# Attention, MLP and routed experts on one core: both ends reordered, and the rows of the position bias dealt out differently

## The chip, the cores and the metric

The program runs on one NeuronCore of a Trainium2 chip. The metric is the device time of one execution in microseconds. The kernel before took 1055.13 us as the median of three runs (1053.98 to 1055.31).

## What is computed

Attention over 4 batches, 8 heads, 576 positions and head size 64, with a bias that depends on the two positions; then an MLP of 512 to 2048 to 512 with the gate h * sigmoid(1.702 h); then a routing of the 2304 tokens to 8 experts with 288 places each and a two-layer expert.

```python
scores = scale * np.matmul(q, k.transpose(0, 1, 3, 2))
psi_rel = np.log1p(np.abs(pos[:, None] - pos[None, :]))
psi_i = np.log1p(np.maximum(pos[:, None], 1.0))
x = (psi_rel / psi_i)[..., None]
bias = np.maximum(x @ w1 + b1, 0.0) @ w2          # 32 hidden units, 8 heads
scores = scores + bias.transpose(2, 0, 1)[None]
attn = softmax(scores);  x = np.matmul(attn, v)
g = h * sigmoid(1.702 * h), h = x @ w_in;  x = g @ w_out
# then each token goes to one of 8 experts: max(x @ w1[e], 0) @ w2[e]
```

## The kernel before

All is fp32. The bias is the same for all batches and is computed once, in 36 **groups** of 64 query positions. In a group the 128 partitions hold 4 positions times 32 hidden units, and there are four **rows** (`row(q, k)`, k = 0 to 3, line 123), each a 128x576 tile: a stretch of the table `lx` (the logarithms times w1), limited from below. A row is made on VectorE (L136, `max` against a column of `psi`) or on ScalarE (L134, Relu with a bias from `bpsi`); the two forms differ by a constant, which `cor` puts back. In the kernel before, ScalarE makes row 0 of the even groups and VectorE the rest: seven rows of a pair of groups on VectorE and one on ScalarE (`alone`, L122).

`prod(q)` (L143, matmuls L151) multiplies the four rows of group q by `w2b` into one two-bank PSUM tile, and `out(q)` (L155, L161 on ScalarE) reads that tile, adds `cor`, scales, and writes a 128x576 staging tile, from which SP's queue scatters it by DMA into the place where the bias waits for its scores (L166, L169). There are 12 row buffers, so a row of group q+3 waits until `prod(q)` has read the buffer, and 7 staging tiles.

The **table** is made at the start: `lx4` (4x1152) is loaded by DMA into a tile P whose borders POOL clears first, three matmuls with `sel` spread it over 128 partitions (L103), and three evictions multiply it by w1 (two on VectorE L107, one on ScalarE L105). Then come `bpsi` and `psi` (L111, L112), and the correction `cor` (four matmuls L116, three small VectorE operations). Ahead of these TensorE runs 12 warm-up matmuls on the identity, which POOL makes.

Attention runs in **slots**, one for each block of up to 128 query rows of a pair of heads (`slot`, L358). The first 20 slots belong to the first four head pairs and batches, in the order block 4 (64 rows, one score tile), then blocks 0 to 3 (two score tiles). One slot issues, each engine taking its own in this order: the transposes of the block three slots back (L294) with three evictions (ScalarE, VectorE, ScalarE); the exponentials of the block before (L257, ScalarE); the output of the last attention product (ScalarE L344, then VectorE L351); the scores of the new block (L237); the bias rows of group q+2 (`rows(0)`); the minimum of scores plus bias for each score tile (L249, VectorE, `least`), which frees the tile; the attention product (L321); then `prod(q)` and `prod(q+1)`, the rows of group q+3 (`rows(1)`) and `out(q)`, `out(q+1)`. Score tiles and bias products share one PSUM pool of two buffers (`sc_ps`). Six groups are multiplied before the first slot (a prologue loop), then two in each of the first 15 slots. Every engine works through its instructions in the order in which they are written; which of the two `sc_ps` buffers a tile gets is chosen when the program is built.

At the **end** the last expert makes its output in four blocks of 128 columns: product, eviction (L1270), three transposes into the banks `ops` (`back`, L1219), then copies into SBUF (`some`, L1230 VectorE and L1232 ScalarE) and three scatters by POOL (`outs`, L1237). For the last expert the copies take columns 0 to 383 after block 2 and 384 to 511 after block 3.

Of the kernel before, what the change touches and what calls it, by code (L numbers as in the profile page):

```python
# [24 lines left out]
NE = 8  # L25
# [39 lines left out]
class Bias:  # L65
# [3 lines left out]
    def __init__(self, net, cst, HL, B4, G9, more, bp, lx4, sc_ps, av_ps):  # L69
# [16 lines left out]
        nc.scalar.dma_start(w1c, bcast_dram(io["w1"], [[0, 4], [1, 32], [1, 1]]))
        nc.sync.dma_start(sel, io["c_sel"])
        nc.scalar.dma_start(b1c, bcast_dram(io["b1"], [[0, 4], [1, 32], [1, 1]]))
        nc.sync.dma_start(psi, bcast_dram(io["psi"], [[4 * NQ, 4], [0, 32], [1, 4 * NQ]]))
        nc.gpsimd.dma_start(w2r, bcast_dram(io["w2"], [[0, 4], [H, 32], [1, H]]))  # L90
# [7 lines left out]

        for c0, c1 in ((0, 320), (320, LXC), (LXC, LXW)):
            sl = slice(c0, c1)  # L100
            ps = sc_ps.tile([128, 2, 512], F32, name="sc")[:, 0, 0:c1 - c0] if c0 < LXC else \
                av_ps.tile([128, 512], F32, name="av")[:, 0:c1 - c0]
            nc.tensor.matmul(ps, sel, lx4[:, sl], start=True, stop=True)  # L103
            if c0 == 320:
                nc.scalar.activation(lx[:, sl], ps, AF.Copy, scale=w1c)  # L105
            else:
                nc.vector.tensor_scalar(lx[:, sl], ps, w1c, None, op0=OP.mult)  # L107
# [6 lines left out]
        cps = av_ps.tile([128, 320], F32, name="av")  # L114
        for k in range(4):
            nc.tensor.matmul(cps[32 * k:32 * k + 32, 0:1], w2b, b1c, start=True, stop=True)  # L116
        nc.vector.tensor_scalar(self.cor[1], cps[:, 0:1], 8.0, None, op0=OP.mult)
        nc.vector.tensor_copy(self.cor[0], self.cor[1])
        nc.vector.memset(self.cor[0][0:32], 0.0)
        self.X, self.PS = {}, {}  # L120

    def alone(self, q):  # L122
        return q % 2
# [54 lines left out]
def attention(net, cst, m, HL, G9, gall):  # L178
# [195 lines left out]

    for k in range(4):
# [4 lines left out]
        if k == 0:  # L380
            lx4 = P[0:4]
# [1029 lines left out]
```

## Time and profile before

| | before |
|---|---|
| median of 3 runs | 1055.13 us (1053.98 to 1055.31) |
| profiled execution | 1055.28 us, its span 1053.5 us, mean granted TensorE clock 0.989 |
| PE busy | 1018.3 us (97% of the span) |
| DVE busy | 704.7 us (67%) |
| ACT busy | 478.4 us (45%) |
| POOL busy | 238.2 us (23%) |

The span runs from the first to the last instruction; the execution is 1.8 us longer than the span. PE is TensorE's matmuls, DVE is VectorE, ACT is ScalarE. Matmuls are pipelined and their ends are modelled, so starts say more than ends. A bracket behind an instruction gives the idle time before it and what ended it.

### The profile page before, as it was taken

To read this page: it belongs to the slowest core of one execution; us is meant where nothing else is said; L and a number is where in the kernel's file an instruction comes from. 1 tells how busy PE (TensorE), PEld (TensorE's weight loads), DVE (VectorE), ACT (ScalarE), POOL (GpSimd) and SP (SyncE) were. 2 spreads that over 40 slices of the span, in tenths; PEclk is the share of its full clock that TensorE was granted. 3 is DMA by queue.
4 is the path that set the end of the run, shared out by engine and by line. 5 is a ranking of instruction groups with operands and counts; after the bars stand their busy time and mean duration, and the time that the engine had idled before them with its cause. 6 is when DMAs were issued, how large, how long until landed. Compare 5 with 4: busy or idle time off the path is not lost.

```text
span 1053.5 us, 19951 instructions
## 1 busy us (share of the span) xinstructions
PE 1018.3 (97%) x7689; PEld 799.3 (76%) x7689; DVE 704.7 (67%) x1838; ACT 478.4 (45%) x1036; POOL 238.2 (23%) x297
## 2 busy tenths in 40 slices
PE   8889999999998989999999999999999999999996
PEld 4455766666665767887777777777777999999996
DVE  6899666666667188874445788888886555555551
ACT  4677776767676223232224322222223455555552
POOL 1122343434344043331113200000001222222111
PEclk8999999999999999999999999999999999999998
DMA  6533422121200255632340272222223755566300
GB/s 185 141 92 100 133 69 71 35 72 35 89 1 1 54 205 210 225 138 103 130 130 17 70 238 83 81 81 81 81 81 133 253 184 184 200 206 205 103 24 23
DMA packets 75747, 119.74 MB, mean 114 GB/s; under 512 B 10340, under 2 KB 38272, under 8 KB 74116
## 3 DMA queue, kind: packets, MB, share of 16 engines
q1 hardware_dynamic: 70156, 104.81, 31.2%
q0 software_dynamic: 3136, 9.46, 2.9%
q10 hardware_dynamic: 2360, 4.20, 1.1%
q8 instruction: 60, 0.98, 0.4%
q14 instruction: 35, 0.29, 0.1%
HBM read 84.24 MB, written 23.60 MB: 102 GB/s over the span
## 4 chain that ended last, share of the span: by engine, by line
PE 68%; issue 19%; DVE 5%; POOL 4%; ACT 2%; DMA 2%; POOLq 0%; SPq 0%; DVEq 0%; ACTq 0%
PE yps L1071 19%; PE hps L609 17%; PE tr L294 8%; PE sc L237 8%; PE av L321 7%; PE sc L151 3%; POOL ye L1189 2%; POOL out_dram L1237 2%; PE rps L843 2%; DVE gall L136 2%; PE lacc L684 1%; DVE P L249 1%; DMA woraw<-in_moe_w_out_dram 1%; PE wps L663 1%; PE av L386 0%
## 5 line engine op out<-in xcount | busy, mean ns | idle before, releaser
L266 POOL TENSOR_SCALAR P<-P,r 128x576 f32<-128x576 f32 x144 | 107.9, 760 | 226.1 <-DVE r L264 164.4
L609 PE MATMUL hps<-xh 128*128 128x512 f32 (+1 forms) x640 | 148.6, 374 | 0.0
L257 ACT ACTIVATE P<-P,nm 128x576 f32<-128x576 f32 x144 | 111.2, 772 | 63.5 <-DVE nm L249 59.8
L609 PEld LDWEIGHTS hps<-xh 128*128 128x128 f32 x640 | 110.3, 188 | 26.9 <-issue 7.5
L1071 PE MATMUL yps<-xh,g 128*128 128x512 f32 x336 | 114.2, 403 | 0.0
L237 PE MATMUL sc<-k,q 64*128 64x288 f32 (+1 forms) x640 | 102.3, 429 | 1.1 <-ACT gall L161 1.1
L294 PEld LDWEIGHTS tr<-ident,P 128*128 128x128 f32 x736 | 79.2, 141 | 31.4 <-issue 25.5
L321 PE MATMUL av<-PT,v 128*64 128x128 f32 (+3 forms) x880 | 95.5, 350 | 4.3 <-DVE xl L351 1.6
L294 PE MATMUL tr<-ident,P 128*128 128x128 f32 x736 | 97.8, 278 | 0.0
L616 DVE TENSOR_TENSOR gall<-hps,sg 128x512 f32<-128x512 f32 (+1 forms) x77 | 48.0, 631 | 71.2 <-ACT sg L615 71.1
L1208 PE MATMUL mps<-xh 128*128 128x288 f32 x288 | 87.3, 303 | 0.0
L321 PEld LDWEIGHTS av<-PT,v 128*64 128x64 f32 x880 | 49.4, 136 | 47.4 <-issue 24.6
L1208 PE MATMUL mps<-xh,xl 128*128 128x288 f32 x288 | 85.1, 295 | 0.0
L1208 PE MATMUL mps<-xl,xh 128*128 128x288 f32 x288 | 84.8, 294 | 0.0
L1071 PE MATMUL yps<-xh 128*128 128x512 f32 x240 | 81.5, 400 | 0.8 <-DVE xh L516 0.8
L615 ACT ACTIVATE sg<-hps 128x512 f32<-128x512 f32 (+1 forms) x77 | 42.3, 551 | 87.8 <-PE hps L609 87.3
L609 PE MATMUL hps<-xl,xh 128*128 128x512 f32 (+1 forms) x320 | 78.9, 368 | 0.0
L270 ACT ACTIVATE PT<-tr 128x384 f32<-128x384 f32 (+2 forms) x176 | 73.0, 423 | 8.3 <-PE tr L294 8.0
L516 DVE TENSOR_TENSOR xl<-wo,xh 128x512 fp32r<-128x512 f32 (+1 forms) x56 | 51.2, 940 | 34.3 <-ACT xh L511 34.2
L237 PEld LDWEIGHTS sc<-k,q 64*128 64x128 f32 (+1 forms) x640 | 54.7, 176 | 25.5 <-issue 11.2
L1071 PEld LDWEIGHTS yps<-xh,g 128*128 128x128 f32 x336 | 63.0, 188 | 13.8
L1208 PE MATMUL mps<-yhi,xh 128*128 128x288 f32 x224 | 68.8, 307 | 0.0
(251 smaller groups left out, 2054.4 us busy)
## 6 DMA issues: line engine op xcount, KB each, us to landing
gd<-gall SPq DMA_DIRECT2D x12, 1152.0 KB, 5.4
woraw<-in_moe_w_out_dram SPq DMA_DIRECT2D x16, 512.0 KB, 5.0
wo<-in_moe_w_dram SPq DMA_DIRECT2D x4, 2048.0 KB, 8.2
gall<-in_moe_w_dram SPq DMA_DIRECT2D x8, 1024.0 KB, 5.0
wiraw<-in_moe_w_in_dram SPq DMA_DIRECT2D x14, 512.0 KB, 5.9
xl<-gd SPq DMA_DIRECT2D x18, 384.0 KB, 4.1
wiraw<-gd SPq DMA_DIRECT2D x18, 384.0 KB, 3.6
wo<-in_moe_w_dram SPq DMA_DIRECT2D x6, 1024.0 KB, 6.7
```

The costliest lines, as they stand in the source:

```text
L237: nc.tensor.matmul(out[:, hf, 0:288], q[rows, icol], k[rows, js[hf]], start=True, stop=True)
L257: nc.scalar.activation(Ps[hh], Ps[hh], AF.Exp, bias=nms[hh], scale=-1.0, accum_out=sums[:, hh:hh + 1])
L266: nc.gpsimd.tensor_scalar(p, p, r[:, hh:hh + 1], 1.0, op0=OP.mult, op1=OP.mult)
L270: nc.scalar.activation(out, in_, AF.Copy)
L294: nc.tensor.transpose(tr[:, k], P[:, c0:c0 + 128], ident)
L321: nc.tensor.matmul(ps[rows, :n], v[:, hh, jt], pt[:, 5 * hh + jt if jt < 4 else 4], start=jt == 0, stop=jt == NIT - 1)
L516: lo_eng.tensor_sub(lo, src, f(hi))
L609: nc.tensor.matmul(ps[:, :n], w[:, c], x[:, c, ts], start=k == 0, stop=k == len(seq) - 1)
L615: nc.scalar.activation(sg[:, :n], ps[:, :n], AF.Sigmoid, scale=1.702)
L616: nc.vector.tensor_tensor(out=self.gall[:, ft % NG, t0:t0 + n], in0=ps[:, :n], in1=sg[:, :n], op=OP.mult)
L1071: nc.tensor.matmul(ps, g[:, ft % 4], w(ft), start=k == 0, stop=k == 47)
L1208: nc.tensor.matmul(ps, w[:, c], x[:, c], start=k == 0, stop=k == len(seq) - 1)
```

## The change

Four edits. First, the start: the small loads are issued before anything else, in another order and on other queues (SP: lx, sel, b1, psi; ScalarE's: w1, w2; POOL's: only ipsi), `lx4` lies in the bias tile of block 4 and not in P, the warm-up matmuls read a tile of ones that VectorE clears, the third eviction of the table is put off to the rows of group 3 (`rest`), and the correction to the rows of group 1, with its PSUM from the pool of the transposes. Second, `alone` is always 0: row 0 of every group is made on ScalarE, so a pair of groups has six rows on VectorE and two on ScalarE. Third, in a slot only rows 0 and 1 of group q+2 are issued ahead of the minimums, and rows 2 and 3 and all of group q+3 behind the products (`part`). Fourth, the end: the last expert's copies are cut at columns 256 and 384, and its last block is transposed into three other PSUM tiles and copied by VectorE (two) and ScalarE (one).

```diff
+        pss = []
         for c0, c1 in ((0, 320), (320, LXC), (LXC, LXW)):
...
+            nc.tensor.matmul(ps, sel, lx4[:, c0:c1], start=True, stop=True)
+            pss.append(ps)
+        nc.vector.tensor_scalar(lx[:, 0:320], pss[0], w1c, None, op0=OP.mult)
+        nc.scalar.activation(lx[:, 320:LXC], pss[1], AF.Copy, scale=w1c)
...
+        def rest():
+            nc.vector.tensor_scalar(lx[:, LXC:LXW], pss[2], w1c, None, op0=OP.mult)
+
+        def correction():
+            cps = tr_ps.tile([128, 4, 128], F32, name="tr").rearrange("p a j -> p (a j)")
+            for k in range(4):
+                nc.tensor.matmul(cps[32 * k:32 * k + 32, 0:1], w2b, b1c, start=True, stop=True)
+            nc.vector.tensor_scalar(self.cor[1], cps[:, 0:1], 8.0, None, op0=OP.mult)
+            nc.vector.tensor_copy(self.cor[0], self.cor[1])
+            nc.vector.memset(self.cor[0][0:32], 0.0)
+        self.later = {1: correction, 3: rest}
...
     def alone(self, q):
-        return q % 2
+        return 0
...
     def rows(self, q):
+        if q in self.later:
+            self.later.pop(q)()
         if q < self.NQ:
             for k in range(4):
                 self.row(q, k)
+
+    def part(self, q, part):
+        for k in range(8):
+            if (k < 2) == (part == 0) and q + k // 4 < self.NQ:
+                self.row(q + k // 4, k % 4)
...
+    small = [B4[0:4, 0:2].rearrange("p h j -> p (h j)")]
+    nc.sync.dma_start(small[0], io["lx"])
+    nc.scalar.dma_start(small[3], bcast_dram(io["w1"], [[0, 4], [1, 32], [1, 1]]))
+    nc.sync.dma_start(small[1], io["c_sel"])
+    nc.sync.dma_start(small[4], bcast_dram(io["b1"], [[0, 4], [1, 32], [1, 1]]))
+    nc.scalar.dma_start(small[5], bcast_dram(io["w2"], [[0, 4], [H, 32], [1, H]]))
+    nc.sync.dma_start(small[2], bcast_dram(io["psi"], [[nq, 4], [0, 32], [1, nq]]))
...
+    nc.vector.memset(pts[0][:, 0:128], 1.0)
     for _ in range(NWARM):
-        nc.tensor.matmul(busy[:, 0:128], ident, ident, start=True, stop=True)
+        nc.tensor.matmul(busy[:, 0:128], pts[0][:, 0:128], pts[0][:, 0:128], start=True, stop=True)
...
-                    rows=lambda k: bias.rows(q + 2 + k), outs=lambda: [bias.out(q + k) for k in range(2)])
+                    rows=lambda k: bias.part(q + 2, k), outs=lambda: [bias.out(q + k) for k in range(2)])
...
+            ps = [t[:, 128 * m:128 * m + 128] for t in OM[e]]
+            if e == NE - 1 and m == 3:
+                ps = [mps.tile([128, 288], F32, name="mps")[0:96, 128 * k:128 * k + 128] for k in (0, 1)]
+                ps.append(tps.tile([128, 288], F32, name="tps")[0:96, 0:128])
...
-                if r == 1:
+                if (r == 1) == (src is None):
                     nc.vector.tensor_copy(o, ps)
...
-                if m == 3 and e == NE - 1:
-                    some(e, 0, 384)
+                if m > 1 and e == NE - 1:
+                    some(e, *((0, 256) if m == 2 else (256, 384)))
...
-        back(NE - 1, 3)
-        some(NE - 1, 384, DM)
+        some(NE - 1, 384, DM, back(NE - 1, 3))
```

## Rows read from the trace of the kernel before

**Rows 1.** Stretches, core 0: length, busy us (instructions) by engine, granted clock, DMA.
```profile
10.00:23.60 13.60, 12.17 (x124) 6.26 (x128) 13.34 (x33) 8.38 (x12) 0.00 (x0) 0.79 0.64 194
23.60:43.86 20.26, 17.01 (x178) 7.93 (x180) 17.51 (x44) 12.54 (x25) 2.47 (x3) 0.92 0.65 176
44.67:106.61 61.94, 55.55 (x692) 34.88 (x692) 57.10 (x150) 46.60 (x101) 13.93 (x19) 1.00 0.37 97
112.24:300.00 187.76, 187.76 (x1451) 121.08 (x1450) 120.50 (x387) 129.02 (x342) 72.72 (x99) 1.00 0.21 66
```

**Rows 2.** Chain that ended last, in one slot: start us, us, what.
```profile
74.09 0.94 DVE gall L136 x2
75.03 0.67 DVE P L249
```

**Rows 3.** Timeline of PE: start us, us, instruction, count, idle before.
```profile
69.46 2.15 PE L151 MATMUL sc<-gall,w2b 128*32 128x288 f32 x32 [0.49 <-DVE nm L249]
72.67 1.24 PE L237 MATMUL sc<-k,q 64*128 64x288 f32 x8
73.84 1.31 PE L321 MATMUL av<-PT,v 128*64 128x128 f32 x20
75.77 2.15 PE L151 MATMUL sc<-gall,w2b 128*32 128x288 f32 x32 [0.61 <-DVE nm L249]
106.61 2.15 PE L151 MATMUL sc<-gall,w2b 128*32 128x288 f32 x32
```

**Rows 4.** Timeline of ACT, the same slot.
```profile
70.78 0.83 ACT L161 ACTIVATE gall<-sc,cor,ipsi 128x576 f32<-128x576 f32 x1 [1.42 <-PE sc L151]
71.68 0.83 ACT L161 ACTIVATE PT<-sc,cor,ipsi 128x576 f32<-128x576 f32 x1
72.41 0.76 ACT L257 ACTIVATE P<-P,nm 128x576 f32<-128x576 f32 x1
73.17 0.26 ACT L344 ACTIVATE xh<-av 128x128 fp32r<-128x128 f32 x1
74.82 0.78 ACT L134 ACTIVATE gall<-gall,bpsi 128x576 f32<-128x576 f32 x1
```

**Rows 5.** Timeline of DVE, the same slot.
```profile
73.46 0.29 DVE L351 TENSOR_TENSOR xl<-av,xh 128x128 fp32r<-128x128 f32 x1
76.96 2.28 DVE L136 TENSOR_SCALAR gall<-gall,psi 128x576 f32<-128x576 f32 x4 [0.31 <-PE sc L151]
```

**Rows 6.** Timeline of the start, PE, SP's queue and DVE.
```profile
1.36 4.83 PE L386 MATMUL av<-ident 128*128 128x128 f32 x24 [1.36 <-POOL ident masks.py:199]
1.51 0.38 SPq L382 DMA_DIRECT2D P<-in_lx_dram  x1
6.96 0.55 DVE L107 TENSOR_SCALAR gall<-sc,w1c 128x320 f32<-128x320 f32 x1 [6.96 <-PE sc L103]
8.36 0.75 DVE L107 TENSOR_SCALAR gall<-av,w1c 128x512 f32<-128x512 f32 x1 [0.84 <-PE av L103]
9.30 0.29 DVE L112 TENSOR_SCALAR psi<-psi,b1c 128x144 f32<-128x144 f32 x1
10.38 12.97 DVE L136 TENSOR_SCALAR gall<-gall,psi 128x576 f32<-128x576 f32 x30
```

**Rows 7.** Timeline: outputs of groups 2 and 3, and the first minimum.
```profile
16.86 1.62 ACT L161 ACTIVATE PT<-sc,cor,ipsi 128x576 f32<-128x576 f32 x2
23.60 0.76 DVE L249 CUSTOM_DVE_ANT_0 P<-sc,b 128x576 f32<-128x576 f32 x1 [0.26 <-DMA xh<-PT]
```

**Rows 8.** Timeline of PE in the first slots.
```profile
23.51 1.18 PE L151 MATMUL sc<-gall,w2b 128*32 128x288 f32 x16 [1.03 <-ACT PT L161]
25.74 2.14 PE L237 MATMUL sc<-k,q 64*64 64x288 f32 x8 [1.05 <-ACT gall L161]
```

**Rows 9.** Timeline of the end, PE and POOL.
```profile
1044.29 0.70 PE L1219 MATMUL ops<-ident,oT 128*96 128x128 f32 x3 [0.60 <-ACT o L1232]
1045.19 0.92 POOL L1237 DMA_INDIRECT out_dram<-o,perm  x1 [21.34 <-ACT o L1232]
```

More of the change, by code (lines that the diff above doesn't have):

```diff
@@ L65, with __init__ @@
 class Bias:
-    def __init__(self, net, cst, HL, B4, G9, more, bp, lx4, sc_ps, av_ps):
+    def __init__(self, net, cst, HL, B4, G9, more, bp, small, sc_ps, av_ps, tr_ps):
         self.net, self.HL, self.B4 = net, HL, B4
@@ L77, in __init__ @@
         lx = self.lx = G9[:, 0:LXW]
-        sel = bp.tile([4, 128], F32, name="sel")
-        psi = self.psi = bp.tile([128, 4 * NQ], F32, name="psi")
+        lx4, sel, psi, w1c, b1c, w2r = small
+        self.psi = psi
         ipsi = self.ipsi = bp.tile([128, NQ], F32, name="ipsi")
-        w1c = bp.tile([128, 1], F32, name="w1c")
-        b1c = bp.tile([128, 1], F32, name="b1c")
         w2b = self.w2b = bp.tile([128, 32], F32, name="w2b")
-        w2r = bp.tile([128, NE], F32, name="w2r")
         nc.gpsimd.memset(w2b, 0.0)
[L86 to L90, printed above, removed]
         nc.gpsimd.dma_start(ipsi, io["ipsi"])
@@ L113, in __init__ @@
         self.cor = [bp.tile([128, 1], F32, name=f"cor{k}") for k in range(2)]
[L114 to L119, printed above, removed]
+        def rest():
[8 more added lines that the diff above has]
+        self.later = {1: correction, 3: rest}
         self.X, self.PS = {}, {}
     def alone(self, q):
-        return q % 2
+        return 0
     def row(self, q, k):
@@ L373, in slot @@
             avq.add(av(*tj))
+    bp = es.enter_context(net.pool("bp", side="right"))
+    nq = 4 * len(GROUPS)
+    small = [B4[0:4, 0:2].rearrange("p h j -> p (h j)")]
+    small += [bp.tile(shape, F32, name=n) for n, shape in (("sel", [4, 128]), ("psi", [128, nq]), ("w1c", [128, 1]),
+                                                           ("b1c", [128, 1]), ("w2r", [128, NE]))]
+    nc.sync.dma_start(small[0], io["lx"])
[4 more added lines that the diff above has]
+    nc.sync.dma_start(small[2], bcast_dram(io["psi"], [[nq, 4], [0, 32], [1, nq]]))
     for k in range(4):
@@ L379, in attention @@
             nc.gpsimd.memset(P[:, c:c + 64], 0.0)
-        if k == 0:
-            lx4 = P[0:4]
-            nc.sync.dma_start(lx4, io["lx"])
     busy = av_ps.tile([128, 320], F32, name="av")
+    pts = [ptp.tile([128, 9 * 320], F32, name="PT") for _ in range(2)]
+    nc.vector.memset(pts[0][:, 0:128], 1.0)
     for _ in range(NWARM):
-        nc.tensor.matmul(busy[:, 0:128], ident, ident, start=True, stop=True)
-    pts = [ptp.tile([128, 9 * 320], F32, name="PT") for _ in range(2)]
+        nc.tensor.matmul(busy[:, 0:128], pts[0][:, 0:128], pts[0][:, 0:128], start=True, stop=True)
     pta = [pts[0][:, 9 * 128 * k:9 * 128 * (k + 1)] for k in range(2)]
     more = [pts[1][:, S * k:S * k + S] for k in range(5)]
-    bp = es.enter_context(net.pool("bp", side="right"))
-    bias = Bias(net, cst, HL, B4, G9, more, bp, lx4, sc_ps, av_ps)
+    bias = Bias(net, cst, HL, B4, G9, more, bp, small, sc_ps, av_ps, tr_ps)
     for pi in range(B):
@@ L1217, in back, with some @@
             o = OT.pop((e, m))
+            ps = [t[:, 128 * m:128 * m + 128] for t in OM[e]]
+            if e == NE - 1 and m == 3:
+                ps = [mps.tile([128, 288], F32, name="mps")[0:96, 128 * k:128 * k + 128] for k in (0, 1)]
+                ps.append(tps.tile([128, 288], F32, name="tps")[0:96, 0:128])
             for r in range(3):
-                nc.tensor.transpose(OM[e][r][:, 128 * m:128 * m + 128], o[:, 96 * r:96 * r + 96], ident)
+                nc.tensor.transpose(ps[r], o[:, 96 * r:96 * r + 96], ident)
+            return ps
         O = {}
-        def some(e, c0, c1):
+        def some(e, c0, c1, src=None):
             if c0 == 0:
@@ L1227, in some @@
             for r in range(3):
-                o, ps = O[e][r][:, c0:c1], OM[e][r][:, c0:c1]
-                if r == 1:
+                o, ps = O[e][r][:, c0:c1], src[r] if src else OM[e][r][:, c0:c1]
+                if (r == 1) == (src is None):
                     nc.vector.tensor_copy(o, ps)
```

6 lines of the change are left out of this document (removed).

## The prediction
> **What bounds the kernel now.** I read the stretches first, then the chain, then the engines' timelines of one slot. From 112 us on TensorE has no idle time at all for 188 us [rows 1], so what is won or lost ahead of that point reaches the end in full, unless a later stage waits for something else. Ahead of it lie three stages where TensorE does not set the pace. In the prologue (10.0 to 23.6) VectorE is busy 13.34 of 13.60 us. In the four slots of block 4 (23.60 to 43.86) it is busy 17.51 of 20.26, and TensorE and ScalarE take turns in waiting. In the next ten slots (44.67 to 106.61, 6.19 us each) VectorE is busy 57.10 of 61.94, TensorE 55.55, ScalarE 46.60 [rows 1]. The chain there runs through bias rows on VectorE, the minimum, and then the products [rows 2]; TensorE stands idle 0.49 to 0.61 us ahead of each pair of products until VectorE's minimum frees the PSUM [rows 3]. So the second and third edits act on the engine that bounds. At the very end the last transposes wait 0.60 us for ScalarE's copies [rows 9].
>
> **The start.** Before, SP's first load waits until 1.51 us for POOL to clear P, and the warm-up matmuls wait 1.36 us for the identity [rows 6]. Both waits go. How much earlier VectorE can have its ones ready is not shown: between 0 and 1.36 us; I take 0.4, since VectorE too has to start up. SP issues one load more (b1) ahead of psi and q and k, ScalarE's queue has w2 in place of b1, POOL's loses w2. None of the landings is shown; the latest moment at which psi and b1 are there is the operation that reads them, at 9.30 us [rows 6]. In order on VectorE, the first eviction starts at 6.96 and the third at 8.36, because the third waits for TensorE; psi follows 0.94 after that start and takes 0.29 [rows 6]. With the third put off, and the first 0.20 shorter, the first row starts 0.94 - 0.20 + 0.30 = 1.04 us after the first eviction: 6.96 - 0.40 + 1.04 = 7.6 us, where it is 9.95 now (one row spacing of 12.97 / 30 = 0.432 ahead of 10.38).
>
> VectorE then makes 12 rows for groups 0 to 3 (14 before) at 0.432, plus the put-off eviction, 0.75, and the correction, 0.36 (9.95 less psi's end at 9.59): 7.6 + 5.18 + 1.11 = 13.9. Group 3's product ends some 0.9 later (half of 2.15 / 2 for what needs the last row, and 70.78 - 69.46 = 1.32 instead of 1.07 until ScalarE sees a product end [rows 3, 4]), its output 0.83 after that: 15.6. Now that output ends at 16.86 + 1.62 = 18.48 and the first minimum starts at 23.60, 5.12 later, ended by a DMA [rows 7]; the same distance gives 20.7. VectorE itself is done with 25 rows (31 before: six go to ScalarE or behind the minimum) at 7.6 + 10.8 + 1.11 = 19.5, which is the other end: 4.1 us won. ScalarE's five rows and three outputs ahead of group 3's output, 5 x 0.69 + 3 x 0.73 = 5.6 us from 7.6, leave it free at 13.2, in time.
> The low end is the clock. The stretch 10.0 to 23.6 has a mean grant of 0.79 [rows 1], so TensorE ran at 1.2 GHz for (1 - 0.79) / 0.5 = 42% of it, 5.7 us. It has little to do between the table's last matmul, whose eviction starts at 8.36, and the first row at 9.95 [rows 6]; in the new order that is from 7.96 to ScalarE's first row at 7.6 + 0.78 = 8.4. If the clock falls all the same, four products of 2.15 us from 8.4 end at 17.0, the output at 18.1, and the minimum comes at 23.2: 0.4 won. I take **2.6 us**, near the upper computation since the idle time is what shrinks.
> The Trainium skill's page "TensorE: Matmul & The Clock Gate" (Part 1, the HAM clock gate) says that the default state is throttled and that activity releases the throttle; the 0.79 agrees with it. By that rule products spread thin over VectorE's row spacing could leave the clock at its lower level, and the sum for the start would be 0.4 and not 2.6.
>
> **The four slots of block 4.** VectorE has six rows a slot and not seven: 4 x 0.43 = 1.7 us less, if it bounds. The half clock costs up to half of (1 - 0.92) / 0.5 x 20.26 = 3.2 us [rows 1], 1.6, and the 2.14 us scores are an example of it [rows 8]. Against this stands a new wait. The row 0 of group q+3 on ScalarE waits for `prod(q)`, because it reuses that group's buffer, and behind it on ScalarE are `out(q)`, `out(q+1)`, the next exponentials and evictions. In these slots `prod(q+1)` and the next scores wait for exactly these outputs (1.03 and 1.05 us [rows 8]), so the row's 0.69 us (from its 0.78 [rows 4], overlap taken off as between two outputs: 72.41 - 71.68 = 0.73) can stand on the path each time: 4 x 0.69 = 2.8 us lost. From 3.3 won to 2.8 lost; I take **0.5 won**, a little to the good of the middle, since VectorE's minimum, now behind one row, can free a PSUM tile before the outputs do.
>
> **The ten slots after.** I set the start of a pair of products to 0, from the slot at 69.46 [rows 3 to 5]. Now: out(q) 1.32, out(q+1) 2.22, exponential 2.95, xh 3.71, xl 4.00, three rows, minimum at 75.03 - 69.46 = 5.57 at the latest, next pair 6.31; scores at 3.21, attention product at 4.38. After: ScalarE's row can start at 1.19, as VectorE's rows of that group do (76.96 - 75.77 [rows 3, 5]); out(q) 1.88, out(q+1) 2.61, ended 3.44; exponential 3.34, xh 4.10, xl 4.39 to 4.68. The scores need both outputs: 3.47 instead of 3.21. The attention product, 1.24 us, needs xl's end and the scores: 4.73. It ends at 5.97. VectorE has one row after xl, then the minimum at about 4.62 + 0.43 = 5.05, and 0.82 later (its 0.76 [rows 7] and 0.06 until TensorE starts, an estimate) a free tile: 5.87. So the pair comes at 5.97: 0.22 a slot less than 6.19, **2.2 us** in ten slots. The new bound is ScalarE's row ahead of the outputs, by way of xh and xl; without it TensorE's own 5.56 (55.55 / 10) would be the floor, 6.3 us won. If the delay of the scores, 0.26, came on top of an unchanged loop, 2.6 us would be lost. The five rows behind the minimums have cover: they must be ready only for the next pair, and 5 x 0.43 from 0.9 ends at 3.1, before VectorE's next eviction matters.
>
> **The end.** The last transposes no longer wait for the copies: 0.60 at most [rows 9]. They still wait for the eviction of the fourth block, and POOL's three scatters keep their pace. Between 0.2 and 0.6; I take **0.5**. The earlier copies at column 256 lie under the products of block 3.
>
> **Sum.** 2.6 + 0.5 + 2.2 + 0.5 = 5.8 us. The profiled execution took 1055.28 us (span 1053.5 and 1.8 around it), 0.15 over the median of the runs shown: 1055.28 - 5.8 - 0.15 = 1049.3 us.
>
> **Rivals.**
> *More than that.* The first slots lose the waits on outputs and the slow clock (2.0), the ten slots come to 5.7 us (4.9), the start gives 3.3, the end 0.5: 10.7, or 1044.4 us. For it: VectorE is at 92% in the ten slots and every other engine has room. Against: ScalarE's outputs end 0.4 us later than now.
> *It hardly does what it says.* The small loads still land late (nothing shows psi and b1 before 9.30 us), or the clock falls: start 0.8. The first slots lose 1.4 to ScalarE's row, the ten win 1.2, the end 0.3: 0.9 won, 1054.2 us.
> *Slower.* ScalarE's row ahead of the outputs closes the loop. Place: every slot with products. Price: 2.8 us in the first four, and in the ten 0.39 each if the row starts only when outputs do now, at 1.32 (scores 3.60 for 3.21): 3.9. With 2.6 and 0.5 won at the ends this is 3.6 lost, 1058.7 us. It decides from the point at which the delay of the scores exceeds TensorE's idle time ahead of the pair. Against it: that idle time is 0.49 to 0.61 [rows 3]. The Trainium skill's page "ScalarE: Activation LUTs" (Rules for kernel authors) has it that relu and max belong on VectorE and not on ScalarE. The rows agree on the price (0.78 against 0.43 spacing); by that rule alone the moved rows would cost 18 x 0.35 = 6.3 us, which holds only where ScalarE is the path.
>
> **Chances.** The forecast 0.56 (its own range 1047.2 to 1051.5), more 0.20, hardly 0.15, slower 0.09. The range that leaves out two in ten goes from 1044.0 to 1054.5. A measurement of this kernel tells 0.2% (2.1 us) from no change: faster than 1053.0 has 0.56 + 0.20 + 0.02 = 0.78, within 0.13, slower 0.09.
>
> **What would show it.** Start: warm-ups before 1.36, the first bias row near 7.6, the first minimum near 21, the granted clock of the prologue above 0.79. First slots: which wait ends before `prod(q+1)`, an output or a minimum, and the time to the first two-tile minimum, 20.26 now. Ten slots: pairs 5.97 apart, TensorE's wait ahead of a pair gone and scores at 3.5 after it, waiting for ScalarE. End: transposes right after the last eviction, the first scatter 0.5 earlier against the last product. The prediction is wrong if the pairs stay 6.2 apart, or if a later stage (weights by DMA, the routing) does not move up with the rest.

## The result, and the profile after

| | before | after |
|---|---|---|
| median | 1054.73 us (4 executions) | 1045.09 us (1043.40 to 1047.58, 4 executions) |
| ratio after to before | | 0.9908, 95% interval 0.9891 to 0.9924 |
| profiled execution, its span | 1055.28, 1053.5 | 1045.06, 1043.3 |
| PE, DVE, ACT busy | 1018.3, 704.7, 478.4 | 1019.5, 697.4, 489.0 |

The kernel became 9.6 us faster; the forecast was 1049.3, the range 1044.0 to 1054.5. The time lies in the range, but 4.2 us under the forecast, and not for the reasons given. TensorE has as many matmuls in both programs, in the same order from the first pair on, so the start of one and the same matmul can be compared in the two profiles:

| stretch | won by the profiles | forecast |
|---|---|---|
| up to the first minimum (23.60, 20.78) | 2.82 | 2.6 |
| four slots of block 4 (to 43.86, 38.84) | 2.20 | 0.5 |
| ten slots, first to last pair (61.94, 59.66) | 2.28 | 2.2 |
| from there to 376 us | -0.37 | 0 |
| first layer of the MLP, 376 to 400 us of before | 3.47 | not seen |
| 746 to 825 us | -0.10 | 0 |
| last eviction to first scatter | -0.14 | 0.5 |
| sum | 10.16 | 5.8 |

The stretches of the kernel after, in the columns of [rows 1] (length, busy us of PE, PEld, DVE, ACT and POOL, granted clock, DMA):

```profile
10.00:20.78 10.78, 10.46 (x117) 4.73 (x109) 10.19 (x24) 8.67 (x14) 0.00 (x0) 0.91 0.71 224
20.78:38.84 18.06, 15.00 (x164) 7.45 (x164) 15.90 (x40) 15.16 (x29) 3.23 (x3) 1.00 0.76 200
39.66:99.32 59.66, 58.81 (x694) 38.59 (x693) 54.50 (x142) 52.65 (x112) 15.70 (x19) 1.00 0.40 104
```

In the ten slots PE is busy 58.81 of 59.66 us, but with the same matmuls that took 55.55 before; it waits inside them. The clock of the first two stretches is 0.91 and 1.00 where it was 0.79 and 0.92. In the slot shown here the chain no longer runs over VectorE [rows 2]; it stays on PE:

```profile
72.55 1.48 PE sc L244 x7
74.03 1.31 PE av L328 x20
```

One of the ten slots on PE, ACT and DVE, against [rows 3 to 5], with an earlier pair on the first line (start, duration, idle before in the bracket):

```profile
45.55 2.15 PE L158 MATMUL sc<-gall,w2b 128*32 128x288 f32 x32 [0.26 <-DVE nm L256]
69.26 2.15 PE L158 MATMUL sc<-gall,w2b 128*32 128x288 f32 x32
72.47 1.55 PE L244 MATMUL sc<-k,q 64*128 64x288 f32 x8
74.03 1.31 PE L328 MATMUL av<-PT,v 128*64 128x128 f32 x20
70.52 0.78 ACT L133 ACTIVATE gall<-gall,bpsi 128x576 f32<-128x576 f32 x1 [0.70 <-PE sc L158]
71.20 1.54 ACT L168 ACTIVATE PT<-sc,cor,ipsi 128x576 f32<-128x576 f32 x2
73.39 0.27 ACT L351 ACTIVATE xh<-av 128x128 fp32r<-128x128 f32 x1
69.93 2.87 DVE L135 TENSOR_SCALAR gall<-gall,psi 128x576 f32<-128x576 f32 x5
73.69 0.29 DVE L358 TENSOR_TENSOR xl<-av,xh 128x128 fp32r<-128x128 f32 x1 [0.42 <-ACT xh L351]
74.32 0.75 DVE L256 CUSTOM_DVE_ANT_0 P<-sc,xh 128x576 f32<-128x576 f32 x1
```

Counted from the pair at 69.26: ScalarE's row 1.26 (forecast 1.19), outputs 1.94 (1.88), xh 4.13 (4.10), xl 4.43 (4.39 to 4.68), minimum 5.06 (5.05), next pair 6.02 (5.97). The idle time ahead of this pair is gone, as foreseen; part of it now lies inside the scores, which take 1.55 us instead of 1.24, since their second tile waits for the second output (it ends at 72.74). In the first three of the ten slots it is not gone: the pairs at 45.55, 51.44 and 57.32 still wait 0.26 us for the minimum, and come 5.88 to 5.89 apart.

The start on DVE and ACT, and the first slots on PE, against [rows 6 to 8]:

```profile
7.65 0.25 DVE L102 TENSOR_SCALAR bpsi<-psi,b1c 128x36 f32<-128x36 f32 x1 [0.39 <-DMA psi<-in_psi_dram]
8.34 1.38 DVE L135 TENSOR_SCALAR gall<-gall,psi 128x576 f32<-128x576 f32 x3
11.94 0.83 ACT L168 ACTIVATE gall<-sc,cor,ipsi 128x576 f32<-128x576 f32 x1 [1.84 <-PE sc L158]
16.11 0.82 ACT L168 ACTIVATE PT<-sc,cor,ipsi 128x576 f32<-128x576 f32 x1
20.78 0.76 DVE L256 CUSTOM_DVE_ANT_0 P<-sc,b 128x576 f32<-128x576 f32 x1 [0.57 <-PE sc L158]
22.29 1.18 PE L158 MATMUL sc<-gall,w2b 128*32 128x288 f32 x16 [1.63 <-ACT PT L168]
24.44 1.19 PE L244 MATMUL sc<-k,q 64*64 64x288 f32 x8 [0.98 <-ACT gall L168]
```

And the end, against [rows 9]: the last eviction of before, then the end after. The wait of the last transposes for ScalarE's copies is gone, and they wait for the eviction alone; but the scatter starts 1.88 us after the eviction, and before it was 1.74:

```profile
1043.45 0.41 ACT L1270 ACTIVATE oT<-mps 128x288 f32<-128x288 f32 x1 [3.12 <-PE mps L1208]
```

```profile
1033.16 0.41 ACT L1292 ACTIVATE oT<-mps 128x288 f32<-128x288 f32 x1 [2.58 <-PE mps L1224]
1033.62 0.42 PE L1240 MATMUL mps<-ident,oT 128*96 128x128 f32 x2 [0.23 <-ACT oT L1292]
1035.04 0.91 POOL L1259 DMA_INDIRECT out_dram<-o,perm  x1 [21.49 <-ACT o L1254]
```

### The profile page after: what moved, and what is told of

It is laid out like the page before. It is cut to its first block, busy times and chain, and to the rows that moved or that the text cites. A ratio compares the mean times of both kernels' runs of the same rounds, so it can differ in the third digit from the quotient of the medians.

```text
span 1043.3 us, 19935 instructions
## 1 busy us (share of the span) xinstructions
PE 1019.5 (98%) x7689; PEld 802.2 (77%) x7689; DVE 697.4 (67%) x1823; ACT 489.0 (47%) x1055; POOL 239.9 (23%) x296
## 3 DMA queue, kind: packets, MB, share of 16 engines
HBM read 84.24 MB, written 23.60 MB: 103 GB/s over the span
## 4 chain that ended last, share of the span: by engine, by line
PE 88%; DVE 3%; issue 3%; DMA 3%; ACT 2%; POOL 1%; SPq 0%; POOLq 0%; DVEq 0%; ACTq 0%
PE yps L1087 18%; PE mps L1224 18%; PE hps L625 17%; PE sc L244 9%; PE av L328 8%; PE tr L301 8%; PE sc L158 3%; PE rps L859 2%; PE lacc L700 1%; PE ops L1240 1%; DMA woraw<-in_moe_w_out_dram 1%; PE tps L1217 1%; DMA xl<-yd,perm 1%; PE wps L679 1%; DMA psi<-in_psi_dram 1%
## 5 line engine op out<-in xcount | busy, mean ns | idle before, releaser
L273 POOL TENSOR_SCALAR P<-P,r 128x576 f32<-128x576 f32 x144 | 110.4, 778 | 216.5 <-DVE r L271 157.3
L244 PE MATMUL sc<-k,q 64*128 64x288 f32 (+1 forms) x640 | 105.3, 426 | 1.5 <-ACT gall L168 1.5
L328 PE MATMUL av<-PT,v 128*64 128x128 f32 (+3 forms) x880 | 95.5, 350 | 4.4 <-DVE xl L358 1.6
L328 PEld LDWEIGHTS av<-PT,v 128*64 128x64 f32 x880 | 49.4, 136 | 47.8 <-issue 24.6
L244 PEld LDWEIGHTS sc<-k,q 64*128 64x128 f32 (+1 forms) x640 | 58.2, 175 | 25.9 <-issue 12.1
```

Of the source, the lines that this page charges most:

```text
L244: nc.tensor.matmul(out[:, hf, 0:288], q[rows, icol], k[rows, js[hf]], start=True, stop=True)
L273: nc.gpsimd.tensor_scalar(p, p, r[:, hh:hh + 1], 1.0, op0=OP.mult, op1=OP.mult)
L328: nc.tensor.matmul(ps[rows, :n], v[:, hh, jt], pt[:, 5 * hh + jt if jt < 4 else 4], start=jt == 0, stop=jt == NIT - 1)
```

## What was tried

Twelve runs in four groups; each ratio is to the kernel before in executions of the same group, whose medians were 1055.84 (`b_flip`, `a_flip`, `b_start`, `a_nhid13`), 1055.15 (`a_alone`, `a_place`, `a_psi_end`, `a_busy`), 1055.81 (`after_again`, `a_best`) and 1056.72 (`a_13_end`, `a_loads`). The names with a begin from the changed kernel.

**The MLP's first layer.** In the kernel before, SP loads `thr` late and TensorE waits twice for the narrowed w_out; after, SP is 10.8 us earlier and one wait is gone. Timelines of before, then of after; the L321 and L328 rows are attention products:

```profile
354.00 2.91 PE L321 MATMUL av<-PT,v 128*64 128x320 f32 x20 [0.94 <-DVE xl L433]
357.01 0.33 SPq L729 DMA_DIRECT2D thr<-in_c_thr_dram  x1
379.33 0.66 PE L663 MATMUL wps<-ident,wo 128*128 128x128 f32 x4 [2.97 <-DVE wo L503]
391.60 0.63 PE L663 MATMUL wps<-ident,wo 128*128 128x128 f32 x4 [1.48 <-DVE wo L503]
```

```profile
345.44 0.65 PE L328 MATMUL av<-PT,v 128*64 128x256 f32 x4
346.19 0.33 SPq L745 DMA_DIRECT2D thr<-in_c_thr_dram  x1
381.25 0.63 PE L679 MATMUL wps<-ident,wo 128*128 128x128 f32 x4 [1.28 <-DVE wo L519]
```

In both programs as built `thr` lies at the same address, inside the second PT buffer. In the kernel before the last PT tile of attention lies there too, so the load, and all of SP's queue behind it with the MLP's weights, waits for the last attention product and leaves 0.10 us after its end (354.00 + 2.91); after, that tile is in the other buffer, and the load leaves 0.10 us after the end of the product before it (345.44 + 0.65). The lower address goes to the tile that is written first, and the ones for the warm-up matmuls now write the first PT tile first.

```diff
 # kernel before, one instruction more (b_flip)
     pts = [ptp.tile([128, 9 * 320], F32, name="PT") for _ in range(2)]
+    nc.vector.memset(pts[0][:, 0:128], 1.0)
 # changed kernel, roles swapped behind its memset and warm-ups (a_flip)
+    pts = pts[::-1]
     pta = [pts[0][:, 9 * 128 * k:9 * 128 * (k + 1)] for k in range(2)]
```

> The kernel before with one VectorE memset of the first PT tile's first 128 columns added at the top; nothing reads the ones. The tile that is written first takes the lower of the two PT buffers, so all later PT tiles swap buffers, and the last PT tile no longer lies over the place of the routing table `thr`. Theory A (the buffer order is what won 3.4 us in the first-layer stage): up to 340 us every start as before, within 0.1 us; SP's load of `thr` starts near 353.2 instead of 357.0; TensorE's waits for the narrowed w_out fall from 4.4 us to about 1.3; all starts from 400 us on are 3.4 us earlier; 1054.7 - 3.4 = 1051.3 us. Theory B (what won it was that the attention stage ended 7 us earlier, ahead of transfers that keep their own time): no change, 1054.7 us.

> The changed kernel with the roles of the two PT tiles swapped (block 4's parts in the second, the five spare rows in the first); instructions and order as they were. Theory A (buffer order): starts up to 340 us as in the changed kernel, `thr` loaded near 350.0 instead of 346.2, TensorE's waits for w_out back at about 4.4 us, 3.4 us lost: 1045.1 + 3.4 = 1048.5 us. Theory B (the earlier end of attention): no change, 1045.1 us.

Measured: 1052.95 us (ratio 0.9978, 0.9960 to 0.9996) and 1048.58 us (0.9929, 0.9913 to 0.9946). All of TensorE's waits from 368 to 410 us (us in total, times, longest), of the kernel before with the memset, then of the changed kernel with the roles swapped:

```profile
PE wps L664 <- DVE wo L504: 0.9, 1, 0.9
```

```profile
PE wps L680 <- DVE wo L520: 4.3, 2, 2.7
```

SP loads `thr` at 354.21 in the first, 0.09 us after the last product but one, and at 352.02 in the second, 0.09 after the last; that is 1.0 and 2.0 later than expected, as the attention of both ended that much later. Between 376 and 400 us the first gained 3.81 us on the kernel before, the second lost 3.26 to the changed one; the two profiles of the question differ by 3.47. Theory A holds: one unread memset is worth this. The totals agree less well: by the ratios the first won 2.3 us on the kernel before and the second lost 2.2 to the change, and the second's interval meets the change's. Other stretches moved: the first also lost 1.6 us between 320 and 340 us, where its profile has a granted clock of 0.51 from 331.2 to 334.7 and that of the kernel before 1.00; the attention product there took 3.41 us instead of 1.83.

**The start edit alone, and the clock.** The changed kernel with the old dealing and the old place of the rows:

```diff
     def alone(self, q):
-        return 0
+        return q % 2
-                    rows=lambda k: bias.part(q + 2, k), outs=lambda: [bias.out(q + k) for k in range(2)])
+                    rows=lambda k: bias.rows(q + 2 + k), outs=lambda: [bias.out(q + k) for k in range(2)])
```

> The changed kernel with the second and third edits undone: bias rows dealt as in the kernel before (ScalarE a row in every second group) and issued ahead of the minimums; the start, the end and the order of the two PT buffers are the changed kernel's. The ten slots should be back at 6.19 us apart in both theories. Theory A (the start edit is worth its own 2.8 us, and the four slots of block 4 gained from the rows): first minimum at 21.0 to 21.6 (two more rows on VectorE ahead of it than in the changed kernel, 0.43 each, hidden or not), the four slots 20.3 us as in the kernel before, total 1054.7 - 2.4 - 3.4 = 1048.9 us. Theory B (the four slots gained because TensorE's clock was up: 1.00 granted against 0.92): the four slots 18.1 to 18.7 us with a grant of 1.00, total 1047 us.

Measured: 1050.80 us (0.9952, 0.9935 to 0.9969). Its ten slots and its four slots:

```profile
42.41:104.35 61.94, 55.56 (x693) 34.86 (x693) 57.14 (x150) 46.65 (x101) 13.96 (x19) 1.00 0.37 98
22.71:41.60 18.89, 15.39 (x175) 7.52 (x177) 17.64 (x45) 12.68 (x26) 3.28 (x3) 1.00 0.70 191
```

The ten slots take what they took before, to the hundredth. The first minimum came at 22.71, later than expected: VectorE makes rows without a pause until then, so of the 2.82 us the start itself is 0.9 and the six rows taken from ahead of the minimum are 1.9. The course of the clock (see below) is alike in `b_start` and the change, but not in the kernel before; against `b_flip` (23.97), where it is alike too, the start gives 1.3. The four slots take 18.89 us with the old rows at a grant of 1.00; with the old rows and 0.92 they took 20.26 [rows 1]. So most of what they won was the clock (theory B, whose 18.1 to 18.7 was a little low). The total fits neither theory well: 0.9952 of 1054.7 is 1049.6 us, against 1048.9 and 1047.

**Each of the two row edits without the other.** `a_alone` undoes the second edit, `a_place` the third (the two hunks above, one at a time).

> The changed kernel with the second edit alone undone: ScalarE makes a row in every second group again, VectorE seven rows a slot, of which one stands ahead of the minimum and six behind it. Theory A (in the ten slots ScalarE's row ahead of the outputs is the path, and VectorE's order, not its load, is what the edits win by): the outputs start 1.3 us after the pair, VectorE's six rows from 0.9 end at 3.5, its copy at 4.1, xl at 4.35, one row, the minimum at 4.8, the pair 0.8 later: 5.6 to 5.8 us apart, less than the 6.01 of the changed kernel; the prologue has six rows more on VectorE, so the first minimum comes at 21.8 to 22.7; total 1045.1 - 3 + 1.2 = 1043.3 us. Theory B (the saving is the row that VectorE no longer makes, 0.43 us a slot): pairs 6.2 us or more apart as before, total 1045.1 + 2.5 + 1.2 = 1048.8 us.

> The changed kernel with the third edit alone undone: ScalarE makes a row in every group, VectorE's six rows of a slot stand three ahead of the minimum and three behind it. Theory A (the two edits are one: VectorE waits for xl, which ScalarE's row makes late, so the rows put behind xl come on top): xl ends 4.7 us after the pair as in the changed kernel, then three rows, the minimum at 5.9, the next pair at 6.7: 7 us lost in the ten slots against the changed kernel, total near 1052 us. Theory B (each edit wins on its own, about 1.1 us in the ten slots): pairs 6.1 us apart, total 1046.3 us.

Measured: 1047.13 us (0.9921, 0.9905 to 0.9938) and 1052.66 us (0.9976, 0.9967 to 0.9986). The ten slots of `a_alone`, then those of `a_place`, then the timeline of its VectorE and PE in one slot:

```profile
42.19:100.86 58.67, 55.77 (x693) 35.32 (x693) 58.15 (x152) 46.61 (x101) 15.80 (x20) 1.00 0.39 103
```

```profile
40.04:106.57 66.53, 59.24 (x692) 38.17 (x692) 52.93 (x140) 52.47 (x111) 13.93 (x19) 1.00 0.35 91
```

```profile
71.33 0.29 DVE L358 TENSOR_TENSOR xl<-av,xh 128x128 fp32r<-128x128 f32 x1 [0.88 <-ACT xh L351]
73.64 2.15 PE L158 MATMUL sc<-gall,w2b 128*32 128x288 f32 x32 [0.65 <-DVE nm L256]
```

| ten slots | rows before the minimum | rows behind it | us |
|---|---|---|---|
| neither edit | 3 | 4 | 61.94 |
| ScalarE's rows only (`a_place`) | 3 | 3 | 66.53 |
| the new place only (`a_alone`) | 1 | 6 | 58.67 |
| both (the change) | 1 | 5 | 59.66 |

Theory A of `a_place` holds: the second edit by itself costs 4.6 us here. VectorE is busy only 52.93 of 66.53 us, sits 0.88 before xl, and then makes three rows while TensorE waits. The third by itself wins 3.3, and the second on top takes 1.0 back. What the second edit gives lies ahead of the ten slots: the first minimum at 20.78 and not 21.83, the four slots in 18.06 and not 19.55. Neither theory of `a_alone` holds in full: the order wins, as A has it, but A had 5.6 to 5.8 a slot; the first pairs are 5.52 and 5.72 apart, the later ones mostly 5.93, and VectorE has hardly any idle time left (busy 58.15 of 58.67).

The Trainium skill's page "ScalarE: Activation LUTs" (Rules for kernel authors) would keep these rows on VectorE. In the ten slots of this pair of kernels that rule holds by 1.0 us, and ahead of them it loses 2.5. With the buffer of the next experiment ScalarE's rows take 55.84 us in the ten slots; how the rows of `a_alone` would do with that buffer was not run.

**The wait of ScalarE's row.** With 12 buffers the row of group q+3 needs the buffer that the product of group q reads. One buffer more (the 19 are shared with the staging of the outputs) and it needs that of group q-1:

```diff
-NHID = 12
+NHID = 13
```

> The changed kernel with 13 buffers for hidden rows instead of 12 and 6 for staging the outputs instead of 7. ScalarE's row of group q+3 then reuses a buffer of group q-1, whose product ran a slot earlier, so the row need not wait for the product of group q. Theory A (this row, standing between the product and the outputs on ScalarE, sets the pace of the slots): ScalarE's wait of 0.70 us ahead of it goes, the outputs start 1.3 us after the pair instead of 1.94, the scores come back to 3.2 after the pair, and the pairs come 5.6 to 5.7 us apart instead of 6.01 (TensorE's own work is 5.56): 3 to 4 us won in the ten slots, 0 to 1 in the four of block 4, total 1045.1 - 3.5 = 1041.6 us. Theory B (VectorE, busy 54.5 of 59.66 us in those slots, sets the pace): pairs stay at 5.9 to 6.0, total 1045.1 us. If six staging buffers are too few, ScalarE's outputs wait for a DMA and the slots get longer: over 1046 us.

Measured: 1042.37 us (0.9874, 0.9858 to 0.9891). Its ten slots, and the timeline of ACT and PE in one (the pair ahead began at 69.55):

```profile
41.83:97.67 55.84, 55.14 (x693) 35.31 (x693) 54.38 (x142) 53.05 (x111) 15.74 (x19) 1.00 0.41 108
```

```profile
69.29 1.45 ACT L133 ACTIVATE gall<-gall,bpsi 128x576 f32<-128x576 f32 x2
70.88 0.83 ACT L168 ACTIVATE gall<-sc,cor,ipsi 128x576 f32<-128x576 f32 x1
75.18 1.18 PE L158 MATMUL sc<-gall,w2b 128*32 128x288 f32 x16
```

Both rows of ScalarE run without a wait, beside the product; the output starts 1.33 after the pair and not 1.94, and the pairs are 5.43 to 5.52, then 5.62 apart. That is 6.1 us less than before in the ten slots; the prediction had named 6.3 as what is left when only TensorE's own work bounds. Theory A holds for the ten slots; VectorE, busy 54.38 of 55.84 us, has little left either. The four slots of block 4 won nothing by it: 19.70 us, against 19.20 in `a_flip` at the same course of the clock.

**Small loads, the end, the clock.** `a_psi_end` deals the loads of b1, psi and w2 anew and has the old dealing of the three last copies (two on ScalarE, the first scatter's among them, and one on VectorE), `a_busy` adds four matmuls on ones:

```diff
 # a_psi_end
-    nc.sync.dma_start(small[4], bcast_dram(io["b1"], [[0, 4], [1, 32], [1, 1]]))
-    nc.scalar.dma_start(small[5], bcast_dram(io["w2"], [[0, 4], [H, 32], [1, H]]))
+    nc.scalar.dma_start(small[4], bcast_dram(io["b1"], [[0, 4], [1, 32], [1, 1]]))
     nc.sync.dma_start(small[2], bcast_dram(io["psi"], [[nq, 4], [0, 32], [1, nq]]))
+    nc.sync.dma_start(small[5], bcast_dram(io["w2"], [[0, 4], [H, 32], [1, H]]))
-                if (r == 1) == (src is None):
+                if r == 1:
 # a_busy: behind the table's three matmuls
+        for _ in range(4):
+            nc.tensor.matmul(fill[:, 0], ones, ones, start=True, stop=True)
```

> The changed kernel with two small edits a millisecond apart, read separately. At the top psi is issued third on SP instead of fourth, b1 goes to ScalarE's queue and w2 to SP's. If psi's landing (VectorE waited 0.39 to 0.84 us for it until 7.65) sets the first row: psi lands 0.6 earlier, VectorE's wait for it goes, the first row starts near 7.9 instead of 8.34 and the first product 0.4 earlier. If the loads queue behind one another whatever their order, the first row stays at 8.3. At the end the last copies of the first scatter's rows are both made by ScalarE, as in the kernel before. If it was VectorE's late copy, waited for in POOL's first wait, 0.56 us ahead of its second, that cost the end its gain: the first scatter starts 1.3 us after the last block's eviction instead of 1.88. If POOL has a delay of its own: 1.8 to 1.9 as now. Total 1045.1 - 0.4 - 0.5 = 1044.2 us, hard to tell from the changed kernel by time alone.

> The changed kernel with four more warm-up matmuls (0.41 us each) on TensorE between the table's matmuls and the first product, where it otherwise does little for 1.3 to 2.2 us. Theory A (the clock falls after that quiet stretch, and what the start wins hangs on it: of three profiled runs of this start one had half the clock for 3 us and two for 7 us and again for 3 us at 24): the granted clock stays at 1.00 from 2 to 44 us, the first minimum comes at 20.2 to 20.5, the four slots take 18.1, total 1044.6 us or a little less with less spread between executions. Theory B (the clock falls at the products, which wait for rows, whatever came before them): the clock falls as before, and the four matmuls delay the first product by up to 0.4 us: 1045.5 us or more.

Measured: 1044.41 us (0.9895, 0.9879 to 0.9912) and 1044.71 us (0.9899, 0.9881 to 0.9916), neither to be told from the change by time. In `a_psi_end` the wait for psi is gone, but not the start's delay; the end has its gain:

```profile
7.02 0.25 DVE L102 TENSOR_SCALAR bpsi<-psi,b1c 128x36 f32<-128x36 f32 x1 [0.27 <-DMA b1c<-in_b_dram]
7.34 1.38 POOL L89 COPY w2b<-w2r 32x8 f32<-32x8 f32 x4 [4.47 <-DMA w2r<-in_w_dram]
8.90 1.64 PE L158 MATMUL sc<-gall,w2b 128*32 128x288 f32 x11
1036.97 0.92 POOL L1259 DMA_INDIRECT out_dram<-o,perm  x1 [20.97 <-ACT o L1254]
```

The first row moved from 8.34 to 7.72, but the first product stayed (8.90 for 8.82): now w2 stood fourth on SP, and POOL's copies of it ended only at 8.72. At the end the last eviction starts at 1035.61, so the scatter follows after 1.36 us; in all eight profiles with the change's dealing it is 1.88 or 1.89, before it was 1.74. The copy that the first scatter waits for ends as long after the eviction in both (1.10 us on VectorE in the change, 1.08 on ScalarE here), so what costs 0.5 us is not when the copy ends but which engine makes it. In the change as built POOL has two waits ahead of this scatter: the first for VectorE's copy and a DMA, the second for ScalarE's copies. In the trace the first ends at 1034.30, as VectorE's copy does, and POOL's queue takes its next step only 0.56 us later; in `a_psi_end` the late copy stands in the second wait, and that step comes 0.05 us after the copy.

In `a_busy` the clock fell all the same (0.50 from 10 to 13 us): theory B. The first product came at 9.71, 0.9 us late and not 0.4; 0.5 of it is that the warm-up matmuls themselves ended later (the table's first matmul at 6.37 instead of 5.88).

> The changed kernel once more, beside the version built from the experiments. Theory A (TensorE's clock in the first 30 us takes one of two courses, whatever the program does): where the warm-up matmuls change from 0.21 to 0.11 us apart before 4.5 us the clock falls near 7.8, stays down 6 to 7 us and falls again near 24, the first minimum comes at 21.3 to 21.6 and everything after it 1.9 us later than in the first profile; where they change after 4.6 us it falls near 8.7 for 3 us and the starts repeat the first profile's within 0.1 us. Theory B (the course belongs to each kernel): the first profile's starts again. Total 1045.1 us by B, 1045 to 1047 by A.

Measured: 1047.11 us (0.9911, 0.9895 to 0.9927). Neither theory: the same program took a third course. Stretches of the change's first profile, then of this one:

```profile
4.00:5.00 1.00, 1.00 (x6) 1.00 (x6) 0.00 (x0) 0.01 (x1) 0.00 (x0) 1.00 0.87 37
9.00:12.00 3.00, 3.00 (x25) 1.91 (x28) 2.92 (x10) 1.16 (x3) 0.00 (x0) 0.50 1.05 404
24.00:27.00 3.00, 2.56 (x32) 1.17 (x36) 1.30 (x6) 2.00 (x5) 0.00 (x0) 1.00 0.66 175
```

```profile
4.00:5.00 1.00, 1.00 (x11) 1.00 (x11) 0.00 (x0) 0.01 (x1) 0.00 (x0) 1.00 0.94 37
9.00:12.00 3.00, 3.00 (x33) 1.34 (x34) 2.92 (x10) 2.13 (x4) 0.00 (x0) 1.00 1.04 402
24.00:27.00 3.00, 2.56 (x12) 0.96 (x16) 0.23 (x2) 1.81 (x4) 0.00 (x0) 0.57 0.65 177
20.23:40.37 20.14, 16.87 (x172) 7.97 (x164) 16.16 (x41) 15.61 (x30) 2.89 (x3) 0.92 0.69 181
```

With the clock up at 9 to 12 us the first minimum came at 20.23, but it fell at 24, and the four slots took 20.14 us. Alike in course, and so comparable: half clock near 10 and again near 24, the kernel before (first minimum 23.60, four slots 20.26) and `a_flip` (21.59, 19.20); a short fall near 10 alone, `b_flip` (23.97, 18.97) and the change (20.78, 18.06). The two stages together won 3.1 to 4.1 us, and the 5.0 of the two profiles holds 0.9 to 2.0 of chance, as far as one profile of each course can tell.

**Putting it together.** `a_best` has 13 buffers, the mended end, b1 on ScalarE's queue and w2 on POOL's; `a_13_end` only the first two; `a_loads` is `a_best` with ipsi on SP behind psi, so that q leaves later.

```diff
 # a_best and a_loads, beside NHID = 13 and the end; a_loads also has the last hunk
-    nc.sync.dma_start(small[4], bcast_dram(io["b1"], [[0, 4], [1, 32], [1, 1]]))
-    nc.scalar.dma_start(small[5], bcast_dram(io["w2"], [[0, 4], [H, 32], [1, H]]))
+    nc.scalar.dma_start(small[4], bcast_dram(io["b1"], [[0, 4], [1, 32], [1, 1]]))
+    nc.gpsimd.dma_start(small[5], bcast_dram(io["w2"], [[0, 4], [H, 32], [1, H]]))
-        nc.gpsimd.dma_start(ipsi, io["ipsi"])
+        nc.sync.dma_start(ipsi, io["ipsi"])
```

> The changed kernel with 13 buffers for hidden rows, the last copies of the first scatter's rows on ScalarE, and the small loads dealt anew: SP has the table, sel and psi, ScalarE's queue w1 and b1, POOL's queue w2 ahead of the clearing of P. If w2 then lands as early as it did from POOL's queue in the kernel before (read at 6.61), the copies of w2 end by 7.5 and no longer hold the first product, as they did when w2 was fourth on SP (7.34 and 8.73): first row at 7.7, first product at 8.1 to 8.3 instead of 8.82, the first minimum 0.3 to 0.5 us earlier than in the changed kernel at the same course of the clock. Pairs 5.52 and then 5.62 us apart, the first scatter 1.36 us after the last eviction. Total 1042.4 (with the 13 buffers alone) - 0.5 - 0.4 = 1041.5 us. If the prologue is set by VectorE's 25 rows and the outputs' transfers and not by its first row, the start gives nothing: 1041.9 us.

> The changed kernel with 13 buffers for hidden rows and the last copies of the first scatter's rows on ScalarE; its loads in its own order. Pairs 5.52 and then 5.62 us apart, the first scatter 1.36 us after the last eviction instead of 1.88, psi read at 7.65. Total 1042.4 (with the 13 buffers alone) - 0.5 = 1041.9 us; by a rival in which the slots' gain is lost again in waits of the last stages for data by DMA, 1043.5 us or more, as in the version with the loads dealt anew.

> The same with the small loads dealt so that the first load of q leaves SP no earlier than in the changed kernel: SP has the table, sel, psi and ipsi ahead of it, ScalarE's queue w1 and b1, POOL's w2. Theory A (b1 was read at 8.87 in the version with the loads dealt anew because q, 288 KB, was issued at 2.23 instead of 2.81 and so ran ahead of it): b1 is read near 7.0 again as when q left at 2.81, w2's copies end by 6.5, the first row comes at 7.7 and the first product at 8.1 to 8.3, 0.6 us ahead of the changed kernel; total 1041.4 us. Theory B (b1 behind w1 on ScalarE's queue is late whenever POOL loads w2): b1 read near 8.9 again, the first product near 10, total 1043 us.

Measured: 1043.48 us (0.9879, 0.9861 to 0.9896), 1041.42 us (0.9853, 0.9832 to 0.9874) and 1040.96 us (0.9855, 0.9837 to 0.9874). SP's first load of q and VectorE's first use of b1, of `a_best`, then of `a_loads`:

```profile
2.23 0.47 SPq L210 DMA_DIRECT2D q<-in_q_dram  x1
8.87 0.25 DVE L102 TENSOR_SCALAR bpsi<-psi,b1c 128x36 f32<-128x36 f32 x1 [1.06 <-DMA b1c<-in_b_dram]
```

```profile
2.75 0.63 SPq L210 DMA_DIRECT2D q<-in_q_dram  x1
7.18 0.24 DVE L102 TENSOR_SCALAR bpsi<-psi,b1c 128x36 f32<-128x36 f32 x1
```

With q issued 0.5 us earlier b1 came at least 1.7 us later, as theory A of `a_loads` has it. Theory B is out, since w2 is on POOL's queue in both. That ipsi moved too is not separated; in `a_psi_end`, with ipsi on POOL's queue and q issued at 2.81, b1 on ScalarE's queue was read at 7.02. The first product came at 8.64 in `a_loads`, not at 8.1 to 8.3: 0.2 us ahead of the change's first profile, whose table started at the same time (5.87 and 5.88). It came at 9.38 in `a_13_end`, where the warm-up matmuls ended later and the table started at 6.48, and at 10.05 in `a_best`. Of the 2.7 us between the profiles of `a_best` and `a_13_end` only 0.9 lie at the start; 0.5 lie in the MLP's first layer and 1.2 between 746 and 825 us. The scatter follows the last eviction after 1.36 to 1.37 us in all three. The last two can't be told apart by time, nor from `a_nhid13` (0.9874), so the total does not show what the mended end is worth; both beat the change, whose interval begins at 0.9891 where theirs end at 0.9874.

## Why the prediction was right or wrong

- **What bounds.** Right: stages ahead of 112 us that VectorE paced, with TensorE waiting for the minimum [rows 3]. "The second and third edits act on the engine that bounds" was half right: the load taken off VectorE alone made the ten slots 4.6 us longer. Its order bounded.
- **The start, 2.6.** Right in sum (2.82), and the reading of 25 rows instead of 31 was what counted. The rest came right by luck. "7.6 us" for the first row failed: 8.34, since psi lands at 7.65; the prediction had said that no landing is shown, and took the earliest. The output of group 3 ended at 16.93, not 15.6. About half of this is the late first row; the rest is ScalarE, which the prediction had free at 13.2, "in time". Its first output waited 1.84 us for a product at half clock, until 11.94, and from there ScalarE made four outputs and three rows without a pause. The distance from there to the minimum was not the 5.12 us carried over from before, but 3.85. Before, VectorE made rows until 23.35, right up to the minimum [rows 6], so the 5.12 measured its rows and not the path of the output. After, its rows end at 20.22 and it waits 0.57 us. The minimum does not read the product that the profile names, and the scores were done at 19.56; what is left is the last scatter of group 3's bias, issued at 17.9. The first two scatters landed 2.4 and 2.6 us after issue, so this one would land near 20.4, an estimate. A group is 16 query positions, 576 in 36 groups, and not 64: groups 0 to 3 make the 64 rows of block 4, which is why the first minimum needs them. So two errors of 1.3 cancelled. The clock's fall, its low end, came in part (0.91).
- **The four slots, 0.5.** Mis-sized: 2.20. The new wait is there, `prod(q+1)` and the scores wait 1.63 and 0.98 at 22.29 and 24.44 where [rows 8] had 1.03 and 1.05, but it fades: in the second slot only the scores wait (0.57 at 28.36), and the later slots run without a stop. At one course of the clock the edits won 0.9 to 1.1, twice what was taken; the rest was the clock.
- **The ten slots, 2.2.** Right, step by step, to 0.1 us in the slot shown; the first three slots are 0.1 shorter and keep a wait for the minimum. So was the bound named, "ScalarE's row ahead of the outputs, by way of xh and xl": taking its wait away gave TensorE's floor. What was not seen is that the second edit costs here.
- **The end, 0.5.** Failed: -0.14. The transposes' 0.60 went [rows 9], PE started right after the eviction, but POOL waited for VectorE's copy in its first wait. With the three last copies dealt as before the end won 0.38 against the old end.
- **Sum.** The number is in the range, but the step that failed most is one that was put at nothing without a reason: stages behind 112 us were to move up with the rest "unless a later stage waits for something else", and nothing in the argument asked what they wait for, or where the tiles lie. The warm-up's ones changed the PT buffers' order, and 3.47 us came from a stage that the diff doesn't touch. "A later stage does not move up with the rest" was named as a sign of error; it moved up more.
- **Rivals.** The time fell near *more than that* (1044.4), though not by its mechanism: the ten slots, its largest term, won 2.3 and not 4.9. *Slower* was a true mechanism at the wrong place: it is what the second edit does without the third. Of *it hardly does what it says* the late loads came in part (psi at 7.65).

## What to carry to other kernels

A tile's first write can decide its address, and an address decides which later load must wait for which last reader: compare the waits of every queue in both programs, in the stages that the diff leaves alone too. Work taken off the bounding engine wins nothing while its order makes another engine wait; find what stands between the product and the next minimum, and give a row that must not wait a buffer of its own. A stage that lives at the edge of the clock needs several profiles before a microsecond of it is put down to an edit.

## What the runs showed of the hardware

- TensorE's warm-up matmuls change from 0.21 to 0.11 us apart at a moment that differs between executions of one program (near 5.2 and 3.9 us in the two of the change; six or eleven matmuls from 4 to 5 us), while the row of the granted clock says 1.00 in both. That 1.00 is no reading: the trace's first record of the clock begins at 5.16 and 3.93, where the spacing changes, and the view fills the time before it. The Trainium skill's page "TensorE: Matmul & The Clock Gate" (Part 1) has the engine begin at the lower level, as the spacing shows. Why one execution then falls to 0.50 near 9 us and another at 24 stays open.
- A load of 512 bytes (b1), issued at 1.94, had landed 5.2 us later when q (288 KB) was issued at 2.75, and was waited for until 6.9 us later when q was issued at 2.23. In this pair of profiles a small load paid for a large one issued right behind it.
- Four loads in a row on SP: whichever stood fourth (psi, 72 KB, or w2, 4 KB, both issued at 2.23) was read at 7.34 to 7.7, its place counting more than its size.
- POOL's wait for another engine's copy cost 0.5 us more where it stood in the first of two waits ahead of a scatter than where it stood in the second (1.88 and 1.36 us from the eviction, in eight and four profiles).
